# Attention and a rational MLP on one core: first keys split over two queues, zero matmuls at the start, half-row stores, and a new order of loads and instructions

## The chip, the cores and the metric

The kernel runs on one core of one Trainium2 chip. The metric is the device time of one launch in microseconds (us), lower is better. Three runs of the kernel before took 445 to 449 us; they count as slow and no ratio uses them. Where this text says "a profiled run" it means the one execution whose trace was taken; its span, from the first to the last instruction, is 1.7 to 1.9 us shorter than the device time of that run.

Engine names are those of the profile: PE is the matrix engine (TensorE) and PEld its weight loads, ACT is ScalarE, DVE is VectorE, POOL is GpSimd and SP is SyncE. A "q" after the name, as in SPq or ACTq, marks the engine's instruction queue, where it issues DMAs. Batches are numbered from 0 to 7 in this text. Times inside a run count from the start of its span.

## The reference, cut to what matters

```python
# q, k, v: (8 batches, 12 heads, 448, 64) float32
scores = (1 / sqrt(64)) * q @ k.T
m = max(scores, axis=-1)
e = exp(scores - m)
attn = e / (sum(e) + exp(-m) + 1e-9)         # "off by one" softmax
x = (attn @ v), heads joined: (3584, 768)
h = x @ w_in                                  # 768 x 2048
P = a0 + a1*h + a2*h**2 + a3*h**3
Q = 1 + |b0|*|h| + |b1|*h**2
out = (P / (Q + 1e-6)) @ w_out                # 2048 x 768, float32
```

Both kernels skip the maximum: exp(s) / (1 + sum exp(s)) is the same value.

## The kernel before

All matmuls are in float16. For each batch, PE computes transposed scores (`sps`), ACT takes the exponentials (`e`), and PE forms the denominators (`den`) and the products with v (`u`). DVE multiplies by the reciprocals, which gives `xt`. PE then does the first large matmul (`hp`), DVE and ACT the rational function, and PE the second large matmul (`op`). Its result is copied to `osb` and stored. Queries and keys must be transposed first. For batches 0 and 1 PE does that (`tq`, `tk`); for batches 2 to 7 it is done by DMA crossbar transposes issued on SP, and the other loads are issued on GpSimd.

The order of instructions on each engine is not written by hand. A class, `Plan`, goes through streams of work with modelled costs. At each step it takes, for each engine, the stream whose next item has the lowest key among those that could start first; on PE a key is raised by a "reluctance" when the item would change the tile shape (reluctance, patience and calm, further down, are its settings):

```python
for eng in cost:
    t = max(self.free[eng], r)
    k = key
    if eng == "PE" and m != mode:
        k += reluctance[self.free["PE"] > calm]
    ahead[eng].append((t, k, s))
# ...
k, t, s = min((k, t, s) for t, k, s in some if t <= soon + ahead_of)
```

So a change of a cost, a key or the load list can re-order every engine's whole program.

The parts that the change touches: the first loads, their casts to float16, the stores, and the keys.

```python
early = {"k": 4, "q": 3}
def load_early(which):
    new_qk(0, which)
    wide[which] = moe.tile([128, DM], F32, tag="osb", name="osb")
    if which == "k":
        for half, eng in enumerate((nc.scalar, nc.sync)):
            eng.dma_start(out=wide["k"][rows(half)].rearrange("p (t x) -> p t x", t=4),
                          in_=of_quad(three(k, 0, half), 0))
        return
    n, w = early[which], NJ * D
    nc.sync.dma_start(out=wide[which][0:T, 0:n * w].rearrange("p (h x) -> p h x", x=w),
                      in_=by_quad(q, 0, 0)[:, 0:n])
# ... (narrow() casts them: keys on DVE, queries on ACT)

osb = osbs[b, tl]                       # a whole output row tile, 128 x 768
copied(eng, osb[:, nh * HD:(nh + 1) * HD], ops.pop((b, tl, nh))[:, 0:HD])
if nh == 1 or last:                     # stored when both halves are there
    store(b, tl * 128, 128, osb, *d)
# ...
first_loads(('k0', 0), ('q0', 0), ('k0', 3), ('q0', 1), ('k0', 1), ('v0', 0), # ...
            ('q2', 2), ('t', 2), ('o', 0), ('v2', 4), ('o', 1), ('g', 2), ('o', 2), ('o', 3))
# ...
S_AT = [0.25, 6.0, 12.0, 16.0, 24.0, 30.0, 36.0, 42.0]     # keys of the scores, by batch
# ... and six more lists of keys
plan.order(0.095, (0.0, 0.5), 0.2, 35.0)
```

In the load list, ('k0', 0) is a part of batch 0's keys, 'w' a piece of w_in, 'o' a piece of w_out, ('t', 2) the crossbar transposes of batch 2, and ('g', 2) a small copy that makes GpSimd wait until those transposes have landed.

The softmax here doesn't subtract the row's maximum and nothing guards it: scores larger than these inputs give would overflow.

## Time and profile before

| | before |
|---|---|
| device time, median of 4 runs | 438.96 us (437.77 to 447.32) |
| span of the profiled run | 436.0 us |
| PE busy | 415.9 us, 95% |
| first transpose on PE | 8.30 us |
| first exponential on ACT | 11.00 us |
| first hp matmul on PE | 40.93 us |
| from there to the end | 395.1 us |

The page of the profiled execution of the kernel before: busy time of each engine, then rows in which each digit is the busy share, in tenths, of one of 40 equal slices (10.9 us each). PEclk is the clock granted to PE, in tenths of full speed.

```profile
span 436.0 us, 8683 instructions
...
PE 415.9 (95%) x3628; PEld 210.2 (48%) x3628; DVE 362.4 (83%) x543; ACT 290.9 (67%) x311; POOL 107.8 (25%) x171
...
PE   1889998999999999999999999999999999999996
...
ACT  1688886689598737767778756667679664675400
...
PEclk9999999999999999999999999999999999999999
```

One of the four runs (447.32 us) is a slow one; the fast three have a median of 438.41 us, and the profiled run (437.8 us) is the fastest of them.

PE is the limit almost everywhere. The exceptions are the first four slices and the last one. The first stretch, up to the first hp matmul, is what this text calls the head.

The waits of PE in the kernel before (engine, tile and line that waited, what released it: total us, times, longest):

```profile
PE sps L385 <- ACT e L395: 5.1, 16, 0.7
PE sps L385 <- DMA qT<-q: 1.2, 1, 1.2
...
```

Sixteen short waits for exponentials, and one wait for a crossbar transpose of batch 2. The timeline of PE in the kernel before (start, duration of the row, engine, line, operation, tiles and shapes, count, and in brackets the idle time before it and its releaser):

```profile
8.30 1.02 PE L277 MATMUL tq<-ident,q 112*128 112x112 f16 x9 [8.30 <-ACT q L136]
...
10.36 0.96 PE L385 MATMUL sps<-qT,kT 64*64 64x448 f16 x8 [0.72 <-DVE kT L291]
...
24.91 0.62 PE L277 MATMUL tq<-ident,q 112*128 112x112 f16 x9
...
40.93 3.57 PE L461 MATMUL hp<-xt,w_in_sb 128*128 128x448 f16 x18
```

Nine transposes of the same shape take 1.02 us at 8.30 and 0.62 us at 24.91. The page's clock row reads 9 throughout, yet the work says that PE ran slower at first. The clock records in the trace begin with a change to full speed at 20.95 us; before the first record the row shows full speed here, whatever is true. So read durations, not that row, at the start of a run. In this text a run is "cold" while PE runs at half clock, which the records of the changed kernel show from 8.76 to 19.00 us (0.50 granted): eight score matmuls take 0.96 us there (at 13.58) and 0.57 us at full clock (at 19.73). They take 0.96 us in the kernel before too, at 10.36.

The timeline of ACT in the kernel before:

```profile
7.41 0.84 ACT L136 ACTIVATE q<-osb 112x768 f16<-112x768 f32 x1 [5.38 <-DMA osb<-in_q_dram]
11.00 2.54 ACT L395 ACTIVATE e<-sps 128x896 f16<-128x896 f32 x3 [2.75 <-PE sps L385]
```

Last, the timeline around the crossbar transposes of batch 3, in the kernel before:

```profile
97.57 0.76 POOL L212 DMA_DIRECT2D v<-in_v_dram  x1
98.77 6.82 SPq L256 DMA_TRANSPOSE qT<-q  x1
99.44 1.35 POOL L179 DMA_DIRECT2D v<-in_v_dram  x2
105.69 4.59 SPq L260 DMA_TRANSPOSE qT<-q  x1
110.37 1.19 SPq L264 DMA_TRANSPOSE qT<-q  x1
```

The duration in an SPq row is the time for which issuing the transfer holds SP's queue, not the time until the data has landed (the first such row ends at 105.6 us, its data landed at 110.1). The view by tile (`--tile qT --engine SP`) gives the landing. The two large transposes hold the queue for 6.82 and 4.59 us and land 11.3 and 6.6 us after their issue, at 110.1 and 112.3 us. The first scores that need them start at about 114.1 us.

### The profile page before, as it was taken

The numbers are of one execution on the slowest core, as the hardware profiler recorded it, in microseconds if no ns is written. First come the engines' busy times: TensorE is split into PE (matmuls) and PEld (weight loads), VectorE is DVE, ScalarE is ACT, GpSimd is POOL, SyncE is SP. The second block draws the span as 40 slices with busy tenths as digits, with TensorE's granted clock in tenths as the row PEclk, the third lists the DMA queues.
The fourth block names the chain that finished last, engine by engine and source line by source line (L and its number), as shares of the span: only waits on it lengthen the run. The fifth ranks groups of instructions, "written<-read, shape, count | busy, mean of one in ns | idle before, by whom it ended". The sixth has DMA issues, their size and how long they took to land.

```text
span 436.0 us, 8683 instructions
## 1 busy us (share of the span) xinstructions
PE 415.9 (95%) x3628; PEld 210.2 (48%) x3628; DVE 362.4 (83%) x543; ACT 290.9 (67%) x311; POOL 107.8 (25%) x171
## 2 busy tenths in 40 slices
PE   1889998999999999999999999999999999999996
PEld 1544444444544455444544454545454455556663
DVE  2334899999999799999989888889989778999821
ACT  1688886689598737767778756667679664675400
POOL 8956214342726070020061002020000000004100
PEclk9999999999999999999999999999999999999999
DMA  9999999999999999311699039710111011102222
GB/s 145 175 180 192 156 112 178 202 184 190 170 204 117 214 192 164 106 38 36 130 193 137 2 99 161 106 37 2 38 38 35 2 38 38 37 2 72 74 72 72
DMA packets 109463, 47.31 MB, mean 109 GB/s; under 512 B 89328, under 2 KB 105968, under 8 KB 109424
## 3 DMA queue, kind: packets, MB, share of 16 engines
q0 software_dynamic: 53776, 22.45, 43.2%
q1 hardware_dynamic: 55296, 24.02, 28.3%
q8 instruction: 28, 0.46, 0.4%
q10 hardware_dynamic: 352, 0.30, 0.3%
q14 instruction: 11, 0.09, 0.1%
HBM read 45.62 MB, written 11.01 MB: 130 GB/s over the span
## 4 chain that ended last, share of the span: by engine, by line
PE 69%; DMA 12%; DVE 9%; POOL 3%; ACT 3%; issue 2%; SPq 2%; DVEq 0%; POOLq 0%
PE op L548 30%; PE hp L461 26%; PE sps L385 6%; PE u L402 5%; DMA q<-in_q_dram 3%; DMA k<-in_k_dram 3%; PE den L402 3%; DMA w_in_sb<-in_moe_w_in_dram 2%; DVE g L138 2%; DMA v<-in_v_dram 1%; SPq L256 1%; DVE w L508 1%; ACT e L395 1%; DVE w L510 1%; POOL k L191 1%
## 5 line engine op out<-in xcount | busy, mean ns | idle before, releaser
L395 ACT ACTIVATE e<-sps 128x896 f16<-128x896 f32 x168 | 146.2, 919 | 56.0 <-PE sps L385 55.8
L461 PE MATMUL hp<-xt,w_in_sb 128*128 128x448 f16 x768 | 158.6, 353 | 0.2 <-DVE g L138 0.2
L548 PE MATMUL op<-w_out_sb,g 128*128 128x384 f16 x768 | 130.7, 326 | 0.0
L461 PEld LDWEIGHTS <-w_in_sb 128*128 128x128 f16 x768 | 70.8, 98 | 76.2 <-issue 17.4
L548 PEld LDWEIGHTS <-g 128*128 128x128 f16 x768 | 73.5, 98 | 53.1 <-issue 5.2
L527 POOL COPY gx<-g 128x256 f16<-128x256 f16 x32 | 20.6, 663 | 244.1 <-DVE g L513 133.5
L515 ACT ACTIVATE c<-c,oneeps_c 128x1792 f16<-128x1792 f16 (+1 forms) x33 | 57.6, 1746 | 29.6 <-DVE c L503 29.4
L138 DVE CAST g<-hp 128x448 f16<-128x448 f32 x107 | 65.9, 618 | 10.9 <-PE hp L461 10.7
L508 DVE TENSOR_TENSOR w<-w,g 128x1792 f16<-128x1792 f16 (+1 forms) x66 | 69.9, 1061 | 0.7
L385 PE MATMUL sps<-qT,kT 64*64 64x448 f16 x672 | 54.3, 374 | 7.3 <-ACT e L395 5.1
L517 ACT ACTIVATE c<-c 128x1792 f16<-128x1792 f16 (+1 forms) x33 | 54.5, 1651 | 0.4
L138 DVE COPY osb<-op 128x384 f32<-128x384 f32 (+1 forms) x51 | 28.2, 552 | 24.4 <-PE op L548 24.4
L510 DVE TENSOR_SCALAR w<-w,abc 128x1792 f16<-128x1792 f16 (+1 forms) x66 | 44.3, 672 | 0.7
L402 PE MATMUL u<-e,v 128*32 128x448 f16 x768 | 40.5, 353 | 0.0
L446 DVE TENSOR_TENSOR xt<-u,rden 128x448 f16<-128x448 f32 x48 | 28.1, 617 | 11.3 <-ACT rden L426 11.1
L385 PEld LDWEIGHTS <-kT 64*64 64x64 f16 x672 | 15.6, 105 | 44.1 <-issue 41.7
L513 DVE TENSOR_TENSOR g<-w,c 128x1792 f16<-128x1792 f16 (+1 forms) x33 | 35.1, 1063 | 1.7 <-ACT e L395 0.5
L503 DVE TENSOR_TENSOR c<-c,w 128x1792 f16<-128x1792 f16 (+1 forms) x33 | 35.1, 1064 | 0.6
L402 PEld LDWEIGHTS <-v 128*32 128x32 f16 x768 | 20.3, 97 | 16.2 <-issue 0.9
L505 DVE TENSOR_SCALAR w<-g,abc 128x1792 f16<-128x1792 f16 (+1 forms) x33 | 24.3, 736 | 0.5
L499 DVE TENSOR_SCALAR c<-w,babs 128x1792 f16<-128x1792 f16 (+1 forms) x33 | 24.1, 730 | 0.4
L402 PE MATMUL den<-e,ones 128*32 128x448 f16 x384 | 22.6, 355 | 0.0
(46 smaller groups left out, 239.3 us busy)
## 6 DMA issues: line engine op xcount, KB each, us to landing
q<-in_q_dram POOLq DMA_DIRECT2D x23, 224.0 KB, 7.5
v<-in_v_dram POOLq DMA_DIRECT2D x14, 288.0 KB, 6.7
k<-in_k_dram POOLq DMA_DIRECT2D x12, 288.0 KB, 9.3
w_in_sb<-in_moe_w_in_dram POOLq DMA_DIRECT2D x16, 192.0 KB, 8.0
w_out_sb<-in_moe_w_out_dram POOLq DMA_DIRECT2D x4, 768.0 KB, 9.7
out_dram<-osb SPq DMA_DIRECT2D x8, 336.0 KB, 2.7
out_dram<-osb SPq DMA_DIRECT2D x8, 288.0 KB, 3.4
out_dram<-osb SPq DMA_DIRECT2D x8, 240.0 KB, 2.6
```

Of the source, the lines that this page charges most:

```text
L138: nc.vector.tensor_copy(out=out, in_=src)
L385: nc.tensor.matmul(out=sps[rows(c), bank, 0:S], lhsT=kT[rows(half), at:at + 64], rhs=qT[rows(half), o:o + S], start=True, stop=True, skip_ ...
L395: nc.scalar.activation(out=e, in_=sps[:, :, 0:S], func=AF.Exp, scale=scale)
L402: nc.tensor.matmul(out=dst[32 * t:32 * t + 32, 0:S], lhsT=lhs(t, slot), rhs=ets[b, qd, i][:, bank, :], start=(n == 0), stop=(n == 3), skip ...
L461: nc.tensor.matmul(out=hp[:, n * w:(n + 1) * w], lhsT=w_in_sb[:, c, fc * 128:(fc + 1) * 128], rhs=xt[:, c, queries(b, z)], start=(c == 0), ...
L503: nc.vector.tensor_tensor(out=c, in0=c, in1=m, op=ALU.mult)
L508: nc.vector.tensor_tensor(out=m, in0=m, in1=h, op=ALU.mult)
L510: nc.vector.tensor_scalar(out=m, in0=m, scalar1=a1 if step == 5 else a0, scalar2=None, op0=ALU.add)
L513: nc.vector.tensor_tensor(out=h, in0=m, in1=c, op=ALU.mult)
L515: nc.scalar.activation(out=c, in_=c, func=AF.Ln, bias=oneeps_c)
L517: nc.scalar.activation(out=c, in_=c, func=AF.Exp, scale=-1.0)
L548: nc.tensor.matmul(out=op[:, 0:HD], lhsT=lhs(fc), rhs=w_out_sb[:, fc, nh * HD:(nh + 1) * HD], start=(fc == 0), stop=(fc == NFC - 1),)
```

## The change

Its intent, from the diff: get the first queries and keys in earlier and in smaller pieces; keep PE busy with zeros while it has nothing else, so that its clock rises early; store each half row as soon as it is ready; let ACT take copies from DVE in nearly all batches (DVE alone did them in batches 0 to 5); and re-tune the list of loads and all keys for that. The core of the diff, with cuts, its load lists put on fewer lines and notes added behind #:

```diff
-    early = {"k": 4, "q": 3}
+    early = {"k": 4, "q": 2}
...
+        nc.sync.dma_start(                         # queries first, two heads
+            out=wide["q"][0:T, 0:n * w].rearrange("p (h x) -> p h x", x=w),
+            in_=by_quad(q, 0, 0)[:, 0:n])
+        for half in range(2):                      # then keys in four pieces
+            load_k(0, half, nc.scalar)
+            load_k(1, half, nc.sync)
...
+    def pieces(b):                                 # first query transposes: 5, then 4, then 8s
+        ends = [0, 5] if b == 0 else [0]
+        ends += [8 * p + 9 for p in range(NP)]
...
+    def busy_work(n):
+        idle = ps.tile([128, 512], F32, tag="gen", bufs=4, name="idle")
+        for _ in range(n):
+            nc.tensor.matmul(out=idle, lhsT=zeros[:, 0:128], rhs=zeros, start=True, stop=True)
...
+        osb = moe.tile([128, HD], F32, tag="osb", name="osb", bufs=4)
...
-        ('v0', 0), ('v0', 3), ('q0', 2), ('k0', 2), ...
+        ('k0', 2), ('k0', 3), ('k0', 1), ('q0', 1), ('q1', 0), ('v0', 0), ('k1', 0), ...
...
+        ('q2', 0), ('v1', 4), ('q2', 1), ('w', 1), ('w', 2), ('w', 3), ('k2', 4), ('q2', 2), ('o', 0), ('t', 2),
         ('v2', 4),
         ('o', 1),
-        ('g', 2),
...
+    add("warm", ("warm", 0), -50, {"PE": (3.87, 3.87)}, lambda: busy_work(9), ...)
...
-    S_AT = [0.25, 6.0, 12.0, 16.0, 24.0, 30.0, 36.0, 42.0]
+    S_AT = [-3.5, 6.5, 11.25, 15.75, 23.5, 29.5, 26.0, 37.0]
...                                                 # and the six other lists of keys
-        copy = {"DVE": (0.534, 0.66), "ACT": (0.43, 0.56)} if b >= 6 else {"DVE": (0.534, 0.66)}
+        copy = {"DVE": (0.534, 0.66), "ACT": (0.43, 0.56)} if b >= 1 else {"DVE": (0.534, 0.66)}
...
-        for t, eng, name, fn in plan.order(0.095, (0.0, 0.5), 0.2, 35.0):
+        for t, eng, name, fn in plan.order(0.095, (0.05, 0.8), 1e-09, 25):
```

Also in it: the transposes of queries and of keys become two streams of the plan rather than one, keys are cast on ACT and queries on DVE (it was the other way round), output copies may go to ACT from batch 2 (was 6), w_out is loaded by column halves, two small constants are loaded over ACT's queue, the load of ACT's function table is issued after the first loads, and the plan is told that PE is free from 1.6 us (was 3.0).

## The prediction

> **What bounds it now.** TensorE: the page of the kernel before gives PE 415.9 of 436.0 us busy. I rebuild that from warm durations in the timeline view: six hp matmuls 1.14 us, sixteen op 2.60, four sps 0.20, sixteen den or u 0.76, a transpose about 0.055. For 768, 896, 672, 1152 and 140 of them: 387 us. The built program changes tile shape 210 times, at about 0.11 us each (a four-matmul sps step between hp groups costs 0.42 us, not 0.20): 23 us. These 410 us stay. The rest:
>
> - Head, about 19 us. The first transpose waits until 8.30 us for the cast of the first queries (wait view), which landed at 7.4. Until about 21 us PE runs at half speed (transposes 0.09 us, an sps step 0.48), though the clock row shows full. [...] ScalarE is only 67 to 74% busy in 10 to 30 us, although its 21 first exponentials (0.81 us each) must end before the first hp matmul, at 40.93 us. PE did about 22 us of warm work by then.
> - Waits after that, about 2.4 us (1.19 on the third batch's crossbar transposes).
> - Tail, 4.4 us after the last matmul.
>
> **What the change does.** (a) Two heads of queries go first on SP (224 KB, not 336), keys in four 96 KB pieces over ACT and SP. [...] an issue here costs 0.4 to 0.8 us, and the gain should come from fewer bytes ahead of the first use. First transposes at about 5.8 us, first exponential at 7.5 (was 11.0). (b) Nine zero matmuls (about 3.8 us cold) fit in the idle start; if PE stays warm, sps steps and transposes halve. (c) Loads ahead of the first w_in piece are the same bytes: it lands near 30 us, the first batch's keys near 10, a stall of 1 to 2 us. ScalarE needs 22 x 0.81 + 3 x 1.05 = 21 us plus stalls: first hp at about 33 us, with 23 us of warm work done. Head waste 10, not 19. (d) 58 of 128 hidden copies (was 21) and 23 output copies (was 5) go to ScalarE. VectorE was 100% busy in 50 to 140 us but hardly limited PE: under 1 us. (e) Shape changes 204: 0.7 us. (f) Half-row stores are off the path; the last store is unchanged. (g) The third batch's transposes are needed later: the 1.19 us wait goes; the fourth batch's become tight.
>
> **Predicted.** 387 + 22.4 + 10 + 2.5 (later stalls) + 4.4 = about 426.5 us span; the time before lies about 2 us above its span: 428.7 us, range 424.5 to 433.5. Faster by over 2%: 0.58; within: 0.40; slower: 0.02.
>
> **Right if** transposes before 15 us last about 0.055 us, the first hp starts at 31 to 35 us, ScalarE is over 80% busy from 8 to 30 us, and PE is full from there to 4.4 us before the end. **Wrong if** PE falls cold again while it waits for keys (2 to 3 us back), first-batch loads land later[...], later batches' clustered sps steps stall on ScalarE, or the fourth batch's transposes arrive after 110 us.

"The third batch" in it is batch 2 and "the fourth batch" is batch 3, in the numbering of this text.

## The result, and the profile after

| | before | after |
|---|---|---|
| device time, median | 438.96 us (437.77 to 447.32, 4 runs) | 432.25 us (432.14 to 432.49, 4 runs) |
| span of the profiled run | 436.0 us | 430.3 us |
| first exponential on ACT | 11.00 us | 8.72 us |
| first hp matmul on PE | 40.93 us | 36.20 us |
| from there to the end | 395.1 us | 394.1 us |

The ratio is 0.9857, with a 95% interval of 0.9832 to 0.9882: a gain of 1.4%, which at a border of 2% is called "same". A ratio is the mean time of one kernel's fast runs over that of the other's fast runs of the same rounds, so it is not quite the ratio of the medians in the table. The means of the fast runs are 438.56 and 432.28 us, 6.3 us apart; the profiled runs explain 5.7 of these, since the one of the kernel before was its fastest. Of the 5.7 us by which the span shrank, 4.7 us (40.93 to 36.20) came before the first hp matmul and 1.0 us after it.

The page of the profiled execution of the changed kernel:

```profile
span 430.3 us, 8847 instructions
...
PE 419.2 (97%) x3637; PEld 211.7 (49%) x3637; DVE 332.8 (77%) x490; ACT 311.9 (72%) x367; POOL 108.5 (25%) x170
...
PE   6999999899999999999999999999999999999996
...
ACT  3688995999937896379864997789998397366300
...
PEclk9699999999999999999999999999999999999999
```

DVE's share fell from 83% to 77% and ACT's rose from 67% to 72%: those are the copies. PE's first slice went from 1 to 6, but much of that is zeros. The clock row now has a 6 in the second slice: PE fell back to half clock. The waits of PE in the changed kernel:

```profile
PE sps L410 <- ACT e L420: 3.0, 6, 1.0
PE tk L298 <- ACT k L135: 1.9, 1, 1.9
...
```

Waits for exponentials fell from 5.1 to 3.0 us and the wait for the crossbar has gone. The timeline of PE in the changed kernel:

```profile
1.20 4.02 PE L312 MATMUL idle<-zeros 128*128 128x512 f16 x9 [1.20 <-DVE zeros L307]
5.01 0.58 PE L288 MATMUL tq<-ident,q 112*128 112x112 f16 x5
7.50 0.34 PE L298 MATMUL tk<-ident,k 128*128 128x128 f16 x3 [1.91 <-ACT k L135]
...
10.21 1.91 PE L298 MATMUL tk<-ident,k 128*128 128x128 f16 x15
11.91 1.70 PE L288 MATMUL tq<-ident,q 112*128 112x112 f16 x16
...
36.20 1.31 PE L486 MATMUL hp<-xt,w_in_sb 128*128 128x448 f16 x6
```

The zeros run, then the first query transposes, and then PE waits 1.91 us for the first keys. The clock records of this run: full from 5.34 us, half from 8.76, full for good from 19.00. The window view of the changed kernel gives ACT's share by stage:

```profile
core 0: us, PE busy (x) PEld busy (x) DVE busy (x) ACT busy (x) POOL busy (x), PEclk, DMA share, GB/s
...
10.00:20.00 10.00, 9.13 (x93) 5.30 (x89) 4.00 (x12) 6.16 (x8) 8.33 (x14) 0.55 1.43 165
20.00:30.00 10.00, 9.67 (x170) 5.44 (x163) 5.97 (x11) 8.87 (x12) 8.43 (x15) 1.00 1.28 157
```

Between 10 and 20 us PE is 91% busy at a mean clock of 0.55, and ACT, whose exponentials set the pace in the head, is only 62% busy. The timeline of ACT in the changed kernel shows where it waited:

```profile
6.92 0.94 ACT L135 ACTIVATE k<-wide 128x384 f16<-128x384 f32 x2 [3.48 <-DMA wide<-in_k_dram]
8.72 2.54 ACT L420 ACTIVATE e<-sps 128x896 f16<-128x896 f32 x3 [0.87 <-PE sps L410]
14.22 3.35 ACT L420 ACTIVATE e<-sps 128x896 f16<-128x896 f32 x4 [2.96 <-PE sps L410]
```

The first exponential came 2.28 us earlier than before (8.72 against 11.00). Then ACT stood for 2.96 us before its fourth (2.16 us at the same place in the kernel before), while PE did 15 and 16 transposes in one go (the rows at 10.21 and 11.91), cold, in 3.4 us (10.21 to 13.61). And the timeline around batch 3's crossbar transposes in the changed kernel:

```profile
97.72 3.32 SPq L263 DMA_TRANSPOSE qT<-q  x1
101.13 3.07 SPq L267 DMA_TRANSPOSE qT<-q  x1
103.03 1.20 POOL L551 COPY gx<-g 128x256 f16<-128x256 f16 x1 [7.18 <-DVE g L538]
104.19 2.56 POOL L211 DMA_DIRECT2D v<-in_v_dram  x2
104.30 1.19 SPq L271 DMA_TRANSPOSE qT<-q  x1
```

GpSimd stood 7.18 us in front of a copy, so its loads came only at 104.19, and the transposes held SP's queue for 3.32 and 3.07 us where it had been 6.82 and 4.59. They landed 5.3 and 6.1 us after their issue (11.3 and 6.6 before), at 103.0 and 107.3 us; the scores that need them start at about 111.7. A slow transpose need not cost time: those of batch 4 in this same run landed 18.6 and 13.1 us after their issue, and PE did not wait for them. There is no gate in the program here any more: the plan placed that copy ahead of the loads in GpSimd's program, and they were issued right after it.

### The profile page after: what moved, and what is told of

The parts are those of the page before. It is cut to its first block, busy times and chain, and to the rows that moved or that the text cites. A ratio compares the mean times of both kernels' runs of the same rounds, so it can differ in the third digit from the quotient of the medians.

```text
span 430.3 us, 8847 instructions
## 1 busy us (share of the span) xinstructions
PE 419.2 (97%) x3637; PEld 211.7 (49%) x3637; DVE 332.8 (77%) x490; ACT 311.9 (72%) x367; POOL 108.5 (25%) x170
## 4 chain that ended last, share of the span: by engine, by line
PE 78%; ACT 14%; DVE 4%; DMA 1%; issue 1%; ACTq 0%
PE op L573 29%; PE hp L486 28%; PE sps L410 8%; ACT e L420 7%; PE u L427 7%; PE den L427 4%; ACT c L540 3%; ACT c L542 2%; PE tq L288 1%; DMA wide<-in_k_dram 1%; PE tk L298 1%; DVE c L528 1%; ACT g L135 1%; ACT rden L448 1%; DVE w L520 1%
## 5 line engine op out<-in xcount | busy, mean ns | idle before, releaser
L486 PE MATMUL hp<-xt,w_in_sb 128*128 128x448 f16 x768 | 153.9, 353 | 0.0
L486 PEld LDWEIGHTS <-w_in_sb 128*128 128x128 f16 x768 | 71.9, 98 | 74.4 <-issue 11.7
L551 POOL COPY gx<-g 128x256 f16<-128x256 f16 x32 | 23.7, 761 | 248.3 <-PE op L573 126.8
L135 ACT ACTIVATE g<-hp 128x448 f16<-128x448 f32 x58 | 31.2, 545 | 38.1 <-PE hp L486 38.1
L137 DVE CAST g<-hp 128x448 f16<-128x448 f32 x70 | 43.2, 618 | 17.7 <-PE hp L486 17.7
L135 ACT ACTIVATE osb<-op 128x384 f32<-128x384 f32 (+1 forms) x24 | 11.9, 494 | 42.4 <-DVE osb L137 23.2
L137 DVE COPY osb<-op 128x384 f32<-128x384 f32 (+1 forms) x33 | 18.2, 552 | 25.6 <-PE op L573 25.5
```

The source lines that it names most:

```text
L135: nc.scalar.activation(out=out, in_=src, func=AF.Copy)
L137: nc.vector.tensor_copy(out=out, in_=src)
L486: nc.tensor.matmul(out=hp[:, n * w:(n + 1) * w], lhsT=w_in_sb[:, c, fc * 128:(fc + 1) * 128], rhs=xt[:, c, queries(b, z)], start=(c == 0), ...
```

## The experiments

The theory after the result had three parts. First, the gain is in the head and comes from the earlier and smaller first pieces; the zeros fail, because PE falls cold again while it waits. Second, half-row stores do nothing. Third, after the head, the re-tuned order and loads keep what was won. Rivals: the zeros make the gain; the second queue makes it; the keys land late because GpSimd's loads run beside them; moving copies to ACT makes it.

Twelve kernels ran, four each on three chips (13, 9, 11 below), with the kernel before beside them. All gave correct results. The spread of the kernel before is wider than most of the differences among the variants, so variants are compared with each other: with the changed kernel, repeated once on chip 13 (432.04 us there, 432.25 in the first look), and with variants of the same chip that turned out to be no different from it. "Full from" is when the clock went to full and stayed there for the head. "Rest" is the span from the first hp matmul to the end.

| run | edit | chip | median (range), us | first exp | full from | first hp | rest |
|---|---|---|---|---|---|---|---|
| r1_changed | none | 13 | 432.04 (430.82 to 432.59) | 9.16 | 13.89 | 35.06 | 394.0 |
| e1_no_zeros | no zeros | 13 | 431.93 (431.23 to 433.35) | 9.04 | 21.97 | 37.59 | 394.0 |
| e2_bridge | eight more zero matmuls | 13 | 431.45 (431.35 to 431.87) | 9.27 | 19.20 | 35.52 | 394.6 |
| e5_before_zeros | kernel before, with zeros | 13 | 438.65 (437.32 to 440.30) | 11.57 | 16.69 | 40.58 | 395.0 |
| e3_one_queue | keys on one queue | 9 | 433.05 (432.21 to 433.54) | 10.09 | 20.36 | 37.50 | 394.2 |
| e4_pool_held | GpSimd's loads after the keys | 9 | 436.13 (435.24 to 436.55) | 8.03 | 23.34 | 39.56 | 394.6 |
| e4b_pool_q | GpSimd's loads after the queries | 9 | 431.97 (430.98 to 432.47) | 8.84 | 13.66 | 34.91 | 394.3 |
| e8_old_loads | old load list | 9 | 440.04 (437.35 to 442.37) | 8.88 | 13.73 | 34.30 | 404.9 |
| e10_filled | zeros in the gaps as well | 11 | 430.26 (429.73 to 430.60) | 9.50 | 4.49 | 34.34 | 394.3 |
| e7_full_rows | old stores | 11 | 431.82 (431.29 to 431.92) | 8.78 | 13.57 | 34.70 | 394.8 |
| e9_old_keys | old keys | 11 | 439.58 (438.31 to 440.99) | 8.87 | 13.72 | 35.94 | 400.6 |
| e6_copies_dve | old places of the copies | 11 | 434.66 (433.89 to 435.62) | 9.67 | 20.15 | 37.18 | 396.3 |

### r1_changed: the changed kernel again

> The changed kernel as it is, for comparison on this chip. Expected by every theory: 432.3 us, span 430.3, first hp matmul at 36.2 us, granted clock full from about 5.5 to 8.9 us, half until about 19 us.

Measured: 432.04 us, ratio 0.981 (0.9757 to 0.9863), so the size of the first look again. But the profiled run had another clock than expected: no early rise, half speed until 13.89 us, then full for good. Its timeline of PE:

```profile
12.22 1.70 PE L288 MATMUL tq<-ident,q 112*128 112x112 f16 x16
13.89 0.57 PE L410 MATMUL sps<-qT,kT 64*64 64x448 f16 x8
```

The sixteen transposes are cold (1.70 us, as in the first look), and the scores after them warm (0.57, where the first look had 0.96). The first hp matmul came 1.1 us earlier than in the first look (35.06 against 36.20). So the clock in the head is not a property of the program: it differs between two executions of the same one.

### e1_no_zeros, e2_bridge and e5_before_zeros: what the zeros do

The first leaves the zeros out of the changed kernel:

```diff
-    add("warm", ("warm", 0), -50, {"PE": (3.87, 3.87)}, lambda: busy_work(9),
+    add("warm", ("warm", 0), -50, {"PE": (3.87, 3.87)}, lambda: busy_work(0),
```

> The changed kernel without its nine zero matmuls. Theory A (the earlier queries and keys gave the head's gain; the zeros bought full clock only for one stretch of 3.4 us, from 5.45 to 8.87 us, because PE then stood idle 1.9 us for the keys): 0.5 to 1.5 us slower than the changed kernel, first hp matmul at 36.5 to 37.5 us. Theory B (the warm-up gave the head's gain): 4 to 6 us slower, near the kernel before.

Measured: 431.93 us against 432.04 for the changed kernel on the same chip. The four runs of each overlap fully. The nine zero matmuls have no effect on the time that these runs can see. Neither theory's time came: the loss of 0.5 to 1.5 us that theory A expected is not there, though the first hp matmul of the profiled run (37.59 us) was as late as it said.

The second puts eight more behind the first query transposes, into the wait for the keys (with all zeros writing one result tile, an edit not shown here):

```diff
         turns[b, p, "q"] = (loaded[b, "qT"][:, g0 * T:g1 * T], tq[:, 0:(g1 - g0) * T])
+        if (b, p) == (0, 0):
+            busy_work(BRIDGE)          # 8
```

> The changed kernel with eight more zero matmuls (1.7 us warm) right after the first transposes of queries, where PE waits 1.9 us for the keys. Theory A: the clock stays full from 5.5 us on, ScalarE's gap of 2.96 us before its fourth exponential halves, first hp matmul at 33 to 34.5 us, time 429.5 to 430.8 us. Rival C (loads of the first batch, not the clock, hold the head): clock full, but first hp matmul still at 36 us and 432.3 us. Rival D (zeros can't hold the clock): half clock from 9 to 19 us as before, 432.3 us.

Measured: 431.45 us, 0.6 us less than the changed kernel, inside its range (430.82 to 432.59). The records show full clock from 5.55 to 15.79 us, then one stretch at half to 19.20. So the bridge carried the clock over the wait for the keys, and it was lost at the next sparse place, where PE waits for exponentials (1.77 us of work from 12.38 to 15.79 us). Theory A, which expected full clock for good, the first hp matmul by 34.5 us and 430.8 us at most, missed all three (first hp at 35.52).

The third puts the zeros into the kernel before and changes nothing else:

```diff
+    zeros = const.tile([128, 512], F16)
+    nc.vector.memset(zeros, 0.0)
+    # ... busy_work as in the change
     load_early("k")
...
+        busy_work(9)
         for t, eng, name, fn in plan.order(
```

> The kernel before with the nine zero matmuls alone. Theory A: the zeros end at about 5.2 us, the first transposes come at 8.3 us, so the clock is half again by 9 to 10 us: within 0.7 us of the kernel before. Theory B: 4 to 5 us faster than the kernel before.

Measured: 438.65 us, ratio 0.9966 (0.9902 to 1.003): no gain that can be told from none, though this interval alone is wide enough for 4 us. The first hp matmul at 40.58 us (40.93 without zeros) shows that the head did not move. This and e1, which without the zeros is still faster than the kernel before (ratio 0.9816, 0.976 to 0.9871), rule out that the zeros made the gain.

### e3_one_queue, e4_pool_held and e4b_pool_q: when the keys land

All key pieces on SP's queue:

```diff
-            load_k(0, half, nc.scalar)
+            load_k(0, half, nc.sync)
```

> The changed kernel with all five early loads issued on SP, one after the other, instead of over SP and ACT. Theory A (a second queue saves issue time only, 0.4 to 0.7 us for each of two issues): the first key piece lands up to 1.3 us later, the last one no later than 0.7 us, so keys are cast at 7.0 to 8.0 us (6.9 in the changed kernel), time 0 to 0.8 us slower than the changed kernel (432.1). Rival E[...]: keys at 9 us or later, time 1.5 to 2.5 us slower.

Measured: 433.05 us; the cast of the first keys started at 7.74 us (6.92 and 6.82 in the two profiles of the changed kernel). Against e4b, on the same chip and no different from the changed kernel, it is 1.1 us slower, and the ranges (432.21 to 433.54, and 430.98 to 432.47) still touch. Theory A has the second queue save the time of issuing. The trace agrees in size: the cast came 0.8 to 0.9 us later, about one issue (the two key issues on ACT's queue took 1.37 us together). So the second queue gives at most about 1 of the some 6 us. The profiled run of e3 also had a late clock (full from 20.36 us, against 13.66 in e4b), so part of this difference can be chance. Rival E, with the keys at 9 us or later, is out.

GpSimd's loads held until the keys have landed, by a tiny copy in front of them that reads the keys:

```diff
     load_early()
+    held = const.tile([128, 2], F16)
+    nc.gpsimd.tensor_copy(out=held, in_=wide["k"][:, 0:DM:HD])
```

> The changed kernel, with GpSimd's loads held until the early keys have landed (a small GpSimd copy reads them first). Theory A (the prediction put the first key transposes at 5.9 us and they came at 7.5[...]): keys land at 5.0 to 5.6 us instead of 6.9, first exponential at 7.0 to 7.8 us instead of 8.7. What follows depends on slack of the other loads: 431 to 432 us if they have slack, slower if the first batch's remaining keys then come 3 us late. Rival F (the keys' time is latency and issue, not sharing): keys still land at 6.5 us or later.

Measured: 436.13 us. The key cast started at 6.23 us, 0.6 to 0.7 us earlier than in the changed kernel, between the two theories. So the loads that were held, when they run beside the keys, cost them that much; two of GpSimd's loads, issued at 1.29 and 2.22 us, still went ahead of the hold, and what those cost is not shown. The loads that were held then came late: PE waited 3.6 us for keys from GpSimd, and the first hp matmul was at 39.56. Holding these loads back for the first keys is a loss here.

A shorter hold, until the queries have landed:

```diff
     load_early()
+    held = const.tile([128, 2], F16)
+    nc.gpsimd.tensor_copy(out=held[0:T, 0:1], in_=wide["q"][0:T, 0:1])
```

> The same, but GpSimd's loads held only until the early queries have landed (3.9 us in the changed kernel). Theory A: keys land at 5.5 to 6.2 us, first exponential at 7.5 to 8.2 us, 431 to 432 us. Rival F: keys as before at 6.9 us.

Measured: 431.97 us, no different from the changed kernel; the key cast started at 6.50 us. It is a weak test: the program that was built issued two of GpSimd's loads, at 1.30 and 2.23 us, ahead of the hold at 3.74 us, so little was held.

### e7_full_rows: the stores

Stores, output tiles and their number as in the kernel before, all else as in the change (the `store` and `outputs` functions shown above):

```diff
-        osb = moe.tile([128, HD], F32, tag="osb", name="osb", bufs=4)
+        if nh == 0:
+            osbs[b, tl] = moe.tile([128, DM], F32, tag="osb", name="osb")
+        osb = osbs[b, tl]
...
-        rings=dict(gen=4, sps=2, e=12, rden=2, g=9, w=2, c=2, xt=2, osb=4, q4=2, k4=2,
+        rings=dict(gen=4, sps=2, e=12, rden=2, g=9, w=2, c=2, xt=2, osb=2, q4=2, k4=2,
```

> The changed kernel with whole-row output buffers and stores as in the kernel before. Theory A: stores are off the path, within 0.8 us of the changed kernel (431.2 to 432.9), first hp unchanged. Rival H (half-row buffers come free sooner, and without them VectorE waits for store transfers, as it did 4.2 us in the run with the old order of loads): 2 us or more slower, with a wait of VectorE for the output transfers.

Measured: 431.82 us. Half-row stores do nothing that can be seen. This also gives the changed kernel a stand-in on chip 11.

### e6_copies_dve: the copies

Hidden and output copies on DVE alone up to batch 5, as before:

```diff
-        copy = {"DVE": (0.534, 0.66), "ACT": (0.43, 0.56)} if b >= 1 else {"DVE": (0.534, 0.66)}
+        copy = {"DVE": (0.534, 0.66), "ACT": (0.43, 0.56)} if b >= 6 else {"DVE": (0.534, 0.66)}
...
-        copy = {"DVE": (0.467, 0.6), "ACT": (0.43, 0.55)} if b >= 2 else {"DVE": (0.467, 0.6)}
+        copy = {"DVE": (0.467, 0.6), "ACT": (0.43, 0.55)} if b >= 6 else {"DVE": (0.467, 0.6)}
```

> The changed kernel, with hidden and output copies of batches 1 to 5 on VectorE alone, as before. Theory A (VectorE hardly limited PE): first hp unchanged, 0 to 1 us slower than the changed kernel. Rival L (the earlier head only counts because VectorE was relieved): first hp unchanged, 3 us or more slower, PE waiting for VectorE after 80 us.

Measured: 434.66 us, 2.8 us more than e7 on the same chip and between the two theories; the rest after the first hp matmul is 396.3 us, 1.5 more than in e7 and 2.3 more than in r1_changed. The remainder is within what the head does by its clock. Apart from the wait for the zeros at the start, PE's waits do not name DVE at all. They name ACT: 4.5 us in 8 waits for exponentials, where the changed kernel has 3.0 in 6. The plan re-orders PE and ACT when the costs change, so this run shows what the permission is worth with this plan's keys. It does not show what a copy costs on either engine.

### e8_old_loads and e9_old_keys: the load list and the keys

The load list of the kernel before in the changed kernel, with its gate:

```diff
         ('q0', 0),
-        ('k0', 2),
         ('k0', 3),
-        ('k0', 1),
         ('q0', 1),
...
-        ('o', 0),
         ('t', 2),
+        ('o', 0),
         ('v2', 4),
         ('o', 1),
+        ('g', 2),
```

> The changed kernel with the order of loads of the kernel before, its gate for two output-weight loads included. Theory A (the order of loads matters only where PE waited for a load: 1.2 us for the third batch's transposes): 0 to 1.5 us slower than the changed kernel; the head unchanged. Rival G (the new order is what brought the first hp matmul forward): first hp matmul 2 us or more later, time 2 to 4 us slower.

Measured: 440.04 us, ratio to the kernel before 0.9991 (0.9918 to 1.0063): the whole gain is gone, far more than either theory allowed. And the head is intact: first hp matmul at 34.30 us. All of the loss is in the rest, 404.9 us against 394.0 in r1_changed. This kernel varies more than the others (437.35 to 442.37 us) and the profiled run took 440.99 us; its fastest run is still 4.9 us above the slowest of e4b on the same chip. The timeline of e8_old_loads, on SP, GpSimd and DVE:

```profile
99.67 2.02 POOL L211 DMA_DIRECT2D v<-in_v_dram  x2
100.95 8.02 SPq L267 DMA_TRANSPOSE qT<-q  x1
...
111.18 7.14 SPq L561 DMA_DIRECT2D out_dram<-osb  x10
...
116.95 0.56 DVE L137 COPY osb<-op 128x384 f32<-128x384 f32 x1 [4.23 <-DMA out_dram<-osb]
```

A transpose issued beside the v loads holds SP's queue for 8.02 us and lands 14.5 us after its issue. The stores wait behind the transposes in SP's queue until 111.18, the output tiles are not free, and DVE stands for 4.23 us. After that the clock records show half speed from 122.96 to 129.79 us. PE's waits in e8_old_loads are longer too:

```profile
PE sps L410 <- ACT e L420: 5.6, 11, 0.9
PE sps L410 <- DMA qT<-q: 2.5, 2, 1.6
PE hp L486 <- DVE xt L471: 2.0, 1, 2.0
```

The changed kernel has 3.0 us of the first and none of the others. The extra waits (2.6, 2.5 and 2.0 us) and at most 3.4 us for the 6.83 us at half speed come to 10.5 of the 10.9 us, by my estimate. Of the 2.5 us for transposes 1.62 are batch 2's and only 0.84 batch 3's; which of the late loads and stores caused the rest is not shown.

The keys, the reluctance, the patience and the calm time of the kernel before, with the new load list:

```diff
-    S_AT = [-3.5, 6.5, 11.25, 15.75, 23.5, 29.5, 26.0, 37.0]
+    S_AT = [0.25, 6.0, 12.0, 16.0, 24.0, 30.0, 36.0, 42.0]
...
-        for t, eng, name, fn in plan.order(0.095, (0.05, 0.8), 1e-09, 25):
+        for t, eng, name, fn in plan.order(0.095, (0.0, 0.5), 0.2, 35.0):
```

> The changed kernel with the scheduling keys of the kernel before (where each batch's stages start, pace, reluctance, patience). Theory A2 (early loads gave 2 us of the head, the new order of the first batch and the clock the rest): first exponential at 8.7 to 9.2 us as in the changed kernel, first hp at 36.5 to 39 us, time 432.5 to 436 us. Rival I (the keys are the gain): 438 us. Rival K (the keys do nothing): 432 us.

Measured: 439.58 us, ratio 1.0004 (0.9938 to 1.0069). Again the head is nearly intact (first hp at 35.94) and the loss is in the rest: 400.6 us, 6.6 more than r1_changed. The timeline of e9_old_keys, on GpSimd, SP and PE:

```profile
96.22 1.69 POOL L211 DMA_DIRECT2D v<-in_v_dram  x2
98.58 8.77 SPq L267 DMA_TRANSPOSE qT<-q  x1
...
114.12 0.96 PE L410 MATMUL sps<-qT,kT 64*64 64x448 f16 x8 [5.17 <-DMA qT<-q]
```

In this order of work GpSimd's copy came sooner, so its loads of v and k were issued from 96.22 to 102.3 us, beside the transposes. One transpose held SP's queue for 8.77 us and landed 15.4 us after its issue, at 113.98; PE stood 5.17 us for it, and after a whole window in which it had done nothing (109.30 to 112.71) its clock was halved for 6.83 us: the eight score matmuls take 0.96 us, not 0.57. The stall and the half clock are large enough together for the loss of 6.6 us: 5.17 us, plus an estimated 3.4 us at most (6.83 us of work that would have taken half as long). The time is above what either A2 or I expected, and the place is another than I's: the keys are not what shortens the head. No run moves only GpSimd's loads, so that they slow the transposes is read from these four profiles and not tested alone: the slowest of batch 3's transposes with these loads beside it landed 11.3 us (before), 14.5 us (e8) and 15.4 us (e9) after its issue, and the large one with none beside it 5.3 us (after).

### e10_filled: a version that keeps the clock

The bridge of e2, and zeros before three score steps in which PE otherwise waits for exponentials:

```diff
+FILL = {2: 3, 5: 3, 6: 1}
...
     def scores(b, qd, i):
+        if (b, qd) == (0, 0) and i in FILL:
+            idles.clear()
+            busy_work(FILL[i])
```

> The changed kernel with the eight bridging zero matmuls and seven more in the gaps where PE waits for ScalarE before the third, sixth and seventh scores steps. So far span = time of the first hp matmul + 394 us in every variant that keeps the order of instructions, and that time follows when the granted clock becomes full for good (13.7 us: hp at 34.9; 19.0: 36.2; 22.0: 37.6). Theory A2: the clock is full from 5 to 8 us on and stays; first hp matmul at 34.0 to 35.0 us, time 429.5 to 431.0 us, and less spread from run to run than the changed kernel. Rival C: hp at 35.5 us or later although the clock is full, 431.5 us or more.

Measured: 430.26 us (429.73 to 430.60), ratio to the kernel before 0.979 (0.9732 to 0.9848). On the same chip e7_full_rows, which differs from the changed kernel in nothing that showed, took 431.82 (431.29 to 431.92): 1.6 us more, and the ranges do not meet. It is the fastest of all that ran, and inside what theory A2 expected. Its clock was full from 4.49 us for good; the mean granted clock was 0.999 or 1.000 in all four of its runs, and 0.989 in three of e7's four. The timeline of PE in e10_filled:

```profile
5.01 1.89 PE L319 MATMUL idle<-zeros 128*128 128x512 f16 x8
...
10.79 1.12 PE L302 MATMUL tk<-ident,k 128*128 128x128 f16 x15
11.84 0.95 PE L290 MATMUL tq<-ident,q 112*128 112x112 f16 x16
...
34.34 1.31 PE L496 MATMUL hp<-xt,w_in_sb 128*128 128x448 f16 x6
```

The 15 and 16 transposes now take 2.0 us in all (10.79 to 12.79), not 3.4, and the first hp matmul is at 34.34 us although the first exponential came later (9.50 against 8.72).

### What the clock records say together

The changes of clock in these runs lie 3.41 us or a multiple apart: 3.41 and 10.24 us in the changed kernel (5.34, 8.76 and 19.00), 10.24 and 3.41 us in e2 (5.55, 15.79 and 19.20), 6.83 us in e8 (122.96 and 129.79). So the runs are read here in windows of 3.41 us, laid from the changes. In e9 the drop follows a window in which PE did nothing (109.30 to 112.71). In the other runs it also came after windows in which PE was not idle: 43% busy (after), 47 and 54% (e4), 48% (e8, 119.55 to 122.96), 52% (e2). But no share of busy time draws the line: the clock stayed full through a window with 53% (e8, 64.93 to 68.35 us). What decides there is not shown. It also stayed full through windows with 59% (e5, 16.69 to 20.10) and 63% (r1, 13.89 to 17.30). What raises the clock is open too: it rose after a window with 83% in e4 (2.86 to 6.27, most of it zeros), and did not rise after windows with 81% in the changed kernel (8.76 to 15.59) and with 87 and 88% in e1 (11.74 to 18.56). The zeros at the start of the changed kernel did not hold: the window after the rise, 5.34 to 8.76 us, with the wait for the keys in it, had 1.47 us of work (43%), and the clock fell. With the bridge of e2 the window after the rise (5.55 to 8.96) had 2.77 us of work (81%), and the clock stayed.

## Why the prediction was right, and which of its terms were off

The time of 432.25 us lies in the range of 424.5 to 433.5, near its slow end, 3.6 us above the predicted 428.7. The prediction gave "faster by over 2%" 0.58 and "within 2%" 0.40; it came out within 2%.

- **What bounds it: right.** The waste was in the head, and 4.7 of the 5.7 us came from there. The reading that PE is cold at the start while the clock row shows full was right, and is confirmed by transposes that take 0.11 us cold and 0.06 us warm (e10).
- **"First hp at about 33 us", "head waste 10, not 19": the term that was mis-sized.** It was 36.20 us, and 35.06 in the second profile. That is 3.2 (2.1) us, nearly all of the miss; the rest after the first hp matmul was 394.1, where the prediction has 393.5 (426.5 minus 33). How far that agreement is luck stays open, since (d) below is a term that the sum left out. Three things make up the 3.2 us; they overlap, and their shares were not measured. The first keys were cast at 6.9 us and the first exponential came at 8.72, not 7.5 us. PE was cold to 19.00 (13.89) us, which (b) made depend on "if PE stays warm", and which "Wrong if" names first, with 2 to 3 us. And the 31 transposes in one go, cold, left a gap of 2.96 us on ACT (2.16 in the kernel before), which the prediction did not see. e10 shows the worth of the warm head: 1.6 us in the medians, 0.9 between the two profiled runs.
- **(a) The queue: right in kind**, since the gain was expected from the bytes ahead of the first use: e3 puts the second queue at about 1 us. "First-batch loads land later": 0.6 to 0.7 us on the keys for the loads that e4 held; two loads were not held.
- **(b) The zeros: "if PE stays warm" did not hold.** They are worth nothing that shows: 432.04 us with them and 431.93 without (e1).
- **(d) "Under 1 us": too low.** Copies on ACT are worth 1.5 to 2.3 us after the first hp matmul in this plan (e6 against e7 and r1_changed); and they relieve waits for exponentials, not DVE. Since e6 re-orders the plan, this is the worth of the permission.
- **(e) Shape changes, 0.7 us:** no run separates this.
- **(f) Stores off the path: right** (e7).
- **(g) Half right.** Batch 2's wait of 1.19 us went. "The fourth batch's become tight" was wrong for the changed kernel: they have about 4.4 us to spare (the second landed at 107.3, the scores start at 111.7), where before they had about 1.8 (112.3 and 114.1). The prediction did not ask what GpSimd would be doing at that time. But the danger it named is real: e9 is the changed kernel with those transposes late, and it loses everything.
- **"ScalarE is over 80% busy from 8 to 30 us": wrong from 10 to 20** (62%; it was 67% before), right from 20 to 30 (89%; 74% before). "PE full from there to 4.4 us before the end": right but for two waits of 1.00 and 0.18 us; the rest of the 3.0 us lies before 24 us.

Where the gain comes from, then: the head. e1, e7, e8 and e9 each take out the zeros, the stores, the new load list or the new keys, and the head stays at 34.3 to 37.6 us in all of them, against 40.6 to 40.9 in both profiles of the old head (before, e5). What is left, and was not taken out alone, is the earlier and smaller first pieces with their finer transposes in two streams, and what the change brought with them: the casts on exchanged engines, the later table load and the new setting for when PE is free. This is an inference by exclusion. How it divides between the earlier arrival (the first exponential 2.3 us earlier) and the finer transposes stays open. The tuned list and keys gain little over the old pair, 1.0 us after the first hp matmul; but either one without the other loses 6.6 (e9) and 10.9 us (e8) there in the profiled runs. The old pair behind the new head was not run, so whether the re-tuning was needed at all stays open too.

## What to carry to other kernels

When an engine order comes from a tuned plan, the load list and the keys fit each other: changing one can cost more than the whole change earns, and one place to look is which bulk loads run beside a transfer that something waits for (here a transpose landed 5.3 us after its issue without them, and the slowest with them 11.3 to 15.4 us). Read when that transfer lands, and not only how long its issue holds the queue. A burst of dummy matmuls did not keep the matrix clock up by itself here: after nine it was full for 3.41 us in one execution (5.34 to 8.76) and not at all before 13.89 us in another (r1); with eight more in the wait that followed it was full from 5.55 to 15.79 us (e2), and with seven more in the next gaps from 4.49 us for good (e10). Whether zeros held is to be read from durations and clock records over several executions, because the clock differs between executions of one program: the changed kernel had it full for good from 19.00 us in one and from 13.89 us in the other. Before crediting a start-up trick, put it alone into the kernel before, and take it alone out of the kernel after; here both runs gave nothing.
